# Moving the gate weights, the slot numbers and the first expert's conversions in an attention + mixture-of-experts + cosine-MLP kernel

## The chip, the cores and the metric

The kernel runs on one core of a Trainium2 chip. The metric is the device time of that core in microseconds (us); lower is better. The core's engines each run their own instruction stream in order: PE (matmuls; PEld is its weight load), DVE, ACT and POOL (elementwise work), and SP, which here only issues DMA loads and stores.

## The reference

Three stages follow each other: attention with queries averaged in pairs, a mixture of eight experts of which each token takes two, and a two-layer network with `h * cos(h)` between its layers. Shapes: 2 batches, 8 heads, 1152 keys, 576 pooled queries, head size 64; so 1152 tokens of 512 values.

```python
q_pool = q.reshape(B, H, S // 2, 2, D).mean(axis=3)
scores = scale * q_pool @ k.transpose(0, 1, 3, 2)
attn = softmax(scores)                       # over 1152 keys
x = (attn @ v).transpose(0, 2, 1, 3).reshape(1152, 512)

noisy = x @ w_gate + np.log1p(np.exp(x @ w_noise)) * noise   # 8 experts
top2 = the two largest of noisy; top2_w = softmax of the two
for e in range(8):                           # tokens that chose e
    out[mask] += top2_w * (np.maximum(x[mask] @ w1[e], 0) @ w2[e])

h = out @ w_in                               # 512 -> 2048
return (h * np.cos(h)) @ w_out               # 2048 -> 512
```

## The kernel before

Every product is done in split precision: a value is written as a high part, rounded to the type that PE multiplies fast, and a low part, the rest. `x_hi` or `conv` writes the high part (on ACT), the line after it the low part (mostly on DVE), and PE runs two or three products in place of one. The order of all work is written out by hand; each engine does its instructions in the order in which the program lists them.

**Attention.** 72 tiles of 128 queries (4 head pairs `hp`, 2 heads `hl`, 9 tiles) run in a loop over `n`. Iteration n emits the scores of tile n + 1 (`s_mm`, L302; maximum on DVE, L312; exponential on ACT, L321), the transposes of tile n (L336) and up to nine matmuls of earlier tiles with V (L374). A transposed tile goes to `eh` and `el` in three parts: two by ACT (L349) and DVE (L353), the third by `t_pool`: ACT copies it to `rw` (L357, two buffers), POOL makes `eh` (L359) and `el` (L360) of it. PE reads these a tile or two later. V is split on POOL too (`split_v`, L117 and L118), from `vn`, which SP loads (L111). What the next head pair needs is spread over the loop by `plan()`, which lists for each n the functions that run first in that iteration: `q_split` on POOL (L145, L147), `q_asm` (L154), `l_asm` (L162), `q_bd` (L170) and `k_asm` (L247), all loads from SP. The tile in the middle of a head (two batches) needs `kb` and `qd`; a head pair begins at n0 = 18 hp.

`load_gate` (L73, L79) runs once, at the end of the prologue: eight POOL instructions put identity blocks into `GW`, and eight loads on SP put the gate's and the noise's weights beside them, 8 columns each, by which `x_group` (L675) multiplies each finished head pair. The last prologue loads stand before it on SP, the loop's first load of `vn` behind it.

**Routing.** After the last tiles `route` runs in two halves, tokens tiles 0 to 3 (`ra`) and 4 to 8 (`rb`). It is a generator; `pump` advances it by a number of steps between other work. Its steps: log-probabilities on ACT and DVE (L467 to L476), the two largest (L479, L482), their one-hot codes `OH` (L484), 128 times the expert (`E128`, L486), the mask `MK` (L488), a matmul that counts earlier tokens of each expert (L496), `KEY` (L498), per token tile a comparison `PM` of the slot numbers with the token's slot in expert 0 (L502), and last the six instructions that work out every token's slot row (L505 to L514). PE then gathers expert 0's tokens with `hot` (L940): eight matmuls of each token tile's high and low parts with its `PM`. PE runs `hot(0, 3)` and `hot(1, 3)` of the first half, then the second half's counting matmul, then the rest.

**Experts.** Step s = 8 e + f handles an eighth of expert e: `h_mm` (twelve matmuls, L1102; ACT makes `hh`, L1113, DVE `hl`, L1114), and `yt_mm` for the step before (twelve matmuls, L1134). Weights come in units: even units 8 e + 2 i hold w1 for two steps, odd ones w2. SP loads a unit into one of three `raw` buffers (`raw_load`, L615 and L619), ACT writes its high part and DVE its low part (`conv`, L625 and L626), and only then is the raw buffer free for the unit three further on. `advance_c(c)` in step s converts up to unit c - 1 and loads up to three more; units 0 to 2 are converted on POOL during attention. The list in the loop gives c for steps 0 to 6, later it is s + 6 (s + 7 at the end). `slot_hots`, `slot_lo` (18 comparisons of DVE, L1064) and `slot_ids` (18 small matmuls, L1071, and six DVE instructions) make the table of which token stands in which slot; from it `x_load` (POOL, L1086) gathers an expert's tokens into three `xr` buffers, and `x_tr` (L1094) transposes them and splits them into `xe`. `yt_evac` copies a finished expert from PSUM (L1143 on ACT, L1145 on DVE), `yt_out` transposes it back (L1151). The last stage's weights come as 64-bit numbers: `dec_load` (L1173, L1175, 1 MB), decoding on DVE (L1182 to L1188) and a store by POOL (L1189), spread over the steps by `DECS`.

## Time and profile before

| | us |
|---|---|
| median of 3 runs | 753.76 (753.61 to 755.12) |
| the profiled execution | 753.42 |
| its span, first to last instruction | 751.8 |
| PE busy in the span | 730.8 |
| DVE busy | 561.8 |
| ACT busy | 519.9 |
| POOL busy | 295.2 |

The page gives the busy time of each engine. A busy PE is not a PE at its peak: its matmuls overlap and their ends are modelled. What is lost on PE shows in two ways, as idle time before an instruction with the name of what ended it, and as a longer distance between the starts of two matmuls than their kind needs. Attention takes about the first 275 us, routing the time to 297, the experts the time to about 545, the last network the rest.

### The profile page before, as it was taken

What the parts mean: (1) busy time and instruction counts of PE and PEld (TensorE: products, weight loads), DVE (VectorE), ACT (ScalarE), POOL (GpSimd) and SP (SyncE); (2) the same over time, 40 slices, a digit from 0 to 9 for tenths busy, and PEclk for the clock granted to TensorE, in tenths of its full rate; (3) what the DMA queues carried; (4) which work ended last, traced back from release to release, by engine and by line L of the source; (5) the groups of instructions that cost most, each with busy time, mean ns of one, the idle gap of its engine ahead of it and who ended that gap; (6) DMA issues with size and microseconds to landing.
All of it is one profiled execution on the core that took longest, in us unless ns stands there. A gap on an engine that the chain in (4) does not pass through costs nothing.

```text
span 751.8 us, 13714 instructions
## 1 busy us (share of the span) xinstructions
PE 730.8 (97%) x4803; PEld 676.7 (90%) x4803; DVE 561.8 (75%) x1176; ACT 519.9 (69%) x1193; POOL 295.2 (39%) x331
## 2 busy tenths in 40 slices
PE   7999999999999998999999999999999999999997
PEld 4789999999999998999999999999888999888885
DVE  5877878877888988868898887776667686656562
ACT  5988789879978963458776675766587675455443
POOL 5978767877877971122010220202177110000000
PEclk9999999999999999999999999999999999999999
DMA  9748667594745510778999999987464100010001
GB/s 219 167 108 214 150 150 164 122 250 98 179 109 171 176 43 19 256 234 287 377 321 348 351 334 325 316 276 236 144 180 137 57 28 1 1 43 0 2 0 60
DMA packets 75329, 125.02 MB, mean 166 GB/s; under 512 B 11950, under 2 KB 42030, under 8 KB 75254
## 3 DMA queue, kind: packets, MB, share of 16 engines
q1 hardware_dynamic: 68678, 101.92, 46.7%
q0 software_dynamic: 5568, 19.14, 7.6%
q10 hardware_dynamic: 1008, 3.02, 1.6%
q8 instruction: 40, 0.66, 0.4%
q14 instruction: 35, 0.29, 0.1%
HBM read 82.15 MB, written 20.33 MB: 136 GB/s over the span
## 4 chain that ended last, share of the span: by engine, by line
PE 77%; DMA 7%; DVE 6%; ACT 4%; POOL 2%; issue 2%; SPq 1%; ACTq 0%; DVEq 0%; POOLq 0%
PE h L1102 17%; PE acc L1102 13%; PE acc L1134 11%; PE s L302 10%; PE pa L374 8%; PE pt L336 8%; PE t L1102 6%; DMA raw<-w_d 2%; DMA qd<-ql 2%; DMA kb<-sh 1%; PE t L1094 1%; PE t L1151 1%; ACT u L625 1%; DMA xr<-x_d,NL 1%; PE pt L675 1%
## 5 line engine op out<-in xcount | busy, mean ns | idle before, releaser
L321 ACT ACTIVATE p<-s,nm 128x384 f32<-128x384 f32 x216 | 126.1, 593 | 0.9 <-DVE nm L314 0.5
L312 DVE TENSOR_REDUCE nm<-s 128x1 f32<-128x384 f32 x216 | 108.4, 550 | 22.9 <-PE s L302 22.3
L1102 PE MATMUL h<-xe,u 128*128 128x320 f32 (+5 forms) x768 | 120.4, 306 | 0.0
L1102 PEld LDWEIGHTS h<-xe,u 128*128 128x128 f32 x768 | 109.8, 189 | 0.5
L626 DVE TENSOR_TENSOR u<-raw,u 128x1024 fp32r<-128x1024 f32 x66 | 81.2, 1233 | 33.5 <-ACT u L625 33.3
L336 PE MATMUL pt<-ident,p 128*128 128x128 f32 x645 | 93.6, 273 | 0.5 <-ACT st L179 0.3
L302 PE MATMUL s<-kt,q 128*128 128x384 f32 x240 | 84.9, 370 | 2.6 <-DVE kt L193 1.3
L374 PE MATMUL pa<-eh,v 128*128 128x320 f32 (+1 forms) x279 | 86.6, 325 | 0.4 <-POOL eh L359 0.4
L625 ACT ACTIVATE u<-raw 128x1024 fp32r<-128x1024 f32 x73 | 77.1, 1058 | 11.3 <-DMA raw<-w_d 5.9
L349 ACT ACTIVATE eh<-pt 128x384 fp32r<-128x384 f32 x144 | 63.0, 492 | 31.1 <-PE pt L336 29.3
L374 PE MATMUL pa<-el,v 128*128 128x320 f32 (+1 forms) x279 | 82.4, 309 | 0.6 <-POOL el L360 0.6
L336 PEld LDWEIGHTS pt<-ident,p 128*128 128x128 f32 x645 | 77.7, 140 | 3.9 <-ACT st L179 0.6
L353 DVE TENSOR_TENSOR el<-pt,eh 128x384 fp32r<-128x384 f32 x144 | 73.1, 549 | 4.4 <-ACT eh L349 2.6
L360 POOL TENSOR_TENSOR el<-rw,eh 128x384 fp32r<-128x384 f32 x71 | 71.6, 1009 | 5.9
L1134 PE MATMUL acc<-hh,u 128*128 128x320 f32 (+5 forms) x448 | 71.8, 303 | 0.0
L1102 PE MATMUL acc<-u,gh 128*128 128x512 f32 x216 | 67.1, 392 | 0.3 <-ACT gh L1470 0.3
L1189 POOL DMA_DIRECT2D w_d<-dw x16 | 9.0, 563 | 148.0 <-DVE dw L1188 148.0
L302 PE MATMUL s<-kt,l 128*128 128x384 f32 x198 | 66.8, 340 | 0.0
L1134 PEld LDWEIGHTS acc<-hh,u 128*128 128x128 f32 x448 | 64.8, 188 | 0.0
L302 PEld LDWEIGHTS s<-kt,q 128*128 128x128 f32 x240 | 44.6, 190 | 11.2 <-ACT p L321 7.6
L374 PEld LDWEIGHTS pa<-el,v 128*128 128x128 f32 x279 | 52.9, 190 | 1.1 <-POOL el L360 1.1
L374 PEld LDWEIGHTS pa<-eh,v 128*128 128x128 f32 x279 | 52.9, 190 | 0.6 <-POOL eh L359 0.6
(285 smaller groups left out, 1599.3 us busy)
## 6 DMA issues: line engine op xcount, KB each, us to landing
raw<-in_moe_w_dram SPq DMA_DIRECT2D x64, 512.0 KB, 5.5
raw<-in_moe_w_in_dram SPq DMA_DIRECT2D x16, 512.0 KB, 7.8
raw<-in_moe_w_out_dram SPq DMA_DIRECT2D x16, 512.0 KB, 7.0
w_d<-dw POOLq DMA_DIRECT2D x16, 512.0 KB, 5.3
raw<-w_d SPq DMA_DIRECT2D x13, 512.0 KB, 3.7
vn<-in_v_dram SPq DMA_DIRECT2D x16, 288.0 KB, 4.9
q<-sh SPq DMA_DIRECT2D x14, 304.0 KB, 3.7
l<-ql SPq DMA_DIRECT2D x14, 304.0 KB, 4.3
```

The source lines that it names most:

```text
L302: nc.tensor.matmul(o, l, r, start=(m == 0), stop=(m == len(mm) - 1))
L312: nc.vector.tensor_reduce(NM[n][:, i:i + 1], SB[n][i][:, 0:384], axis=AX.X, op=OP.max, negate=True)
L321: nc.scalar.activation(P[n][i], SB[n][i][:, 0:384], AF.Exp, bias=NM[n][:, 3:4], accum_out=SUMS[:, t, 2 * hp + hl, i:i + 1])
L336: nc.tensor.transpose(p[:, c], P[n][j][:, c], ident)
L349: nc.scalar.activation(t_dst(n, j)[0], t_src(n, j), AF.Copy)
L353: nc.vector.tensor_tensor(el, t_src(n, j), ef, op=OP.subtract)
L360: nc.gpsimd.tensor_tensor(el, rw, ef, op=OP.subtract)
L374: nc.tensor.matmul(st["p"][:, 0:w], V2[hp, hl, b][:, VC[c] if hp + b else c, :], (EH, EL)[s][:, c, EB[g]:EB[g] + w], start=(c == 0 and s = ...
L625: nc.scalar.activation(b[:, 0], r, AF.Copy)
L626: st_w["lo"].tensor_tensor(b[:, 1], r, b.bitcast(F32)[:, 0], op=OP.subtract)
L1102: nc.tensor.matmul(o, l, r, start=first and i == 0, stop=last and i == len(seq) - 1)
L1134: nc.tensor.matmul(ACC[e, d][:, 0:CAPS[e]], w[:, i, 128 * d:128 * d + 128], r[:, 0:CAPS[e]], start=f == 0 and r is hh and i == 0, stop=f = ...
```

## The change

- `load_gate` leaves the end of the prologue and becomes the last event of iteration 8 in `plan()`, behind `q_split(1)`.
- `l_asm(hp, 1)` and `q_bd(hp, 1)` run in iteration n0 + 1 and no more in n0, so behind `k_asm(hp, 1)`.
- In `route` the product `E128` and the slot rows leave; a new function `slot_rows` does them once for all nine token tiles, right before `slot_hots`. For it ACT copies the counts from PSUM into `LG`, whose first eight columns are free by then. The `PM` comparisons of token tiles 1 to 3 move from DVE to POOL.
- `slot_lo` runs in steps 1 to 3 with three token tiles each; it ran in steps 0 to 3 with 3, 3, 2 and 1.
- `slot_ids` and `x_load(1)` run in step 4 ahead of the conversions and no more at its end.
- The conversions of steps 0 to 4 are one a step (units 3 to 7), two each in steps 5 and 6; they were 2, 0, 2, 1, 1, 1 and 2.
- The last product of expert 0, `yt_mm(0, 7)`, runs between the second and third transposes of expert 1 and no more ahead of them.
- `yt_evac(1)` is done by ACT alone.
- The second `dec_load` moves from step 3 to step 6.
- From expert 1 on `x_load(e + 2)` runs at f = 6, right after the transposes that free its buffers, and no more at the end of f = 7.

```diff
@@
                                 I8[:, ts, 0:2, None].to_broadcast([128, nt, 2, 8]), op=OP.is_equal)
-        nc.vector.tensor_scalar(E128[:, ts], I8[:, ts, 0:2], 128.0, None, op0=OP.mult)
         yield
@@
         nc.vector.scalar_tensor_tensor(KEY[:, ts], MK[:, ts, 0], -4096.0, pp[:, :, 0], op0=OP.mult, op1=OP.add)
+        nc.scalar.activation(LG[:, ts, 0:8], pp, AF.Copy)
         yield
@@
             PM[t] = xs.tile([128, CAP], F32R, name="pm", bufs=9)
-            nc.vector.tensor_scalar(PM[t], IOTAC, KEY[:, t:t + 1], None, op0=OP.is_equal)
+            eng = nc.gpsimd if 0 < t < 4 else nc.vector
+            eng.tensor_scalar(PM[t], IOTAC, KEY[:, t:t + 1], None, op0=OP.is_equal)
             yield
+
+    def slot_rows():
+        nt, ts = NT, slice(0, NT)
+        nc.vector.tensor_scalar(E128, I8[:, :, 0:2], 128.0, None, op0=OP.mult)
         tmp = OHP[:, ts]
-        nc.vector.tensor_tensor(tmp, OH[:, ts], pp[:, :, None, :].to_broadcast([128, nt, 2, 8]), op=OP.mult)
+        nc.vector.tensor_tensor(tmp, OH, LG[:, :, None, 0:8].to_broadcast([128, nt, 2, 8]), op=OP.mult)
         pj, pi = PJ[:, ts], PI[:, ts]
         nc.vector.tensor_reduce(pj, tmp, axis=AX.X, op=OP.add)
-        yield
         nc.vector.tensor_copy(pi, pj)
         nc.vector.scalar_tensor_tensor(pj, pj, 8.0, E128[:, ts], op0=OP.mult, op1=OP.add)
-        yield
         nc.vector.tensor_scalar(pi, pi, 127, None, op0=OP.bitwise_and)
-        yield
-        nc.vector.scalar_tensor_tensor(ROW[:, ts], pi, -7.0, pj, op0=OP.mult, op1=OP.add)
-        yield
+        nc.vector.scalar_tensor_tensor(ROW, pi, -7.0, pj, op0=OP.mult, op1=OP.add)
 
@@
                 at(m + 9 + d, q_asm, hp, 1, False)
-                at(n0, l_asm, hp, 1)
-                at(n0, q_bd, hp, 1)
                 for j in range(3):
@@
                 at(m + 18, k_asm, hp, 1)
+                at(n0 + 1, l_asm, hp, 1)
+                at(n0 + 1, q_bd, hp, 1)
+        at(8, load_gate)
         return ev
@@
     q_bd(0, 1)
-    load_gate()
 
@@
     def slot_lo(i):
-        for t in range((0, 3, 6, 8)[i], (3, 6, 8, 9)[i]):
+        for t in range(3 * i, 3 * i + 3):
             for j in range(2):
@@
             o = ACC.pop((e, d))[:, 0:n]
-            if d % 2 == 0:
+            if d % 2 == 0 or e == 1:
                 nc.scalar.activation(t[:, d, 0:n], o, AF.Copy)
@@
     CD = 5
-    DL = (1, 3)
+    DL = (1, 6)
     DECS = {}
@@
         DECS.setdefault(DL[i], []).append(lambda i=i: dec_load(i))
+    slot_rows()
     slot_hots()
@@
                 x_tr(e + 1, f - 3)
+                if f == 6 and e + 2 < E_N:
+                    x_load(e + 2)
             elif not e and f == 7:
-                yt_mm(0, 7)
                 for kd in range(4):
+                    if kd == 2:
+                        yt_mm(0, 7)
                     x_tr(1, kd)
@@
                 yt_evac(0)
+            if s == 4:
+                slot_ids()
+                x_load(1)
             if s < NCONV - 1:
-                advance_c((5, 5, 7, 8, 9, 10, 12)[s] if s < 7 else s + LA + (s > 58))
+                advance_c((4, 5, 6, 7, 8, 10, 12)[s] if s < 7 else s + LA + (s > 58))
             for c in DECS.get(s, []):
@@
             if not last:
-                if s < 4:
-                    slot_lo(s)
-                if (e, f) == (0, 4):
-                    slot_ids()
-                    x_load(1)
-                elif e and f == 7 and e + 2 < E_N:
-                    x_load(e + 2)
+                if 0 < s < 4:
+                    slot_lo(s - 1)
     for st in range(2):
```

## Rows read from the trace of the kernel before

**Rows 1.** Busy us of each engine in 38 windows of 20 us: their sum.
```profile
sum 760.00, PE 730.75 PEld 676.73 DVE 561.80 ACT 519.92 POOL 295.16; mean PE 19.23 PEld 17.81 DVE 14.78 ACT 13.68 POOL 7.77
```

**Rows 2.** PE's waits, by line and releaser: us in total, times, longest.
```profile
PE s L496 <- DVE MK L488: 1.0, 1, 1.0
...
PE pt L940 <- DVE pm L502: 0.8, 1, 0.8
PE acc L1134 <- DVE hl L1114: 0.7, 1, 0.7
PE s L302 <- DMA kb<-sh: 0.7, 2, 0.5
PE t L1094 <- DVE xe L989: 0.7, 1, 0.7
PE pa L374 <- POOL el L360: 0.6, 2, 0.3
PE t L1151 <- DVE yt L1145: 0.5, 1, 0.5
...
PE pa L374 <- POOL eh L359: 0.4, 1, 0.4
...
PE t L1094 <- DMA xr<-x_d,NL: 0.3, 1, 0.3
```

**Rows 3.** Timeline of PE, routing: start, us, instruction, count, idle before and releaser.
```profile
290.47 0.31 PE L940 MATMUL pa<-pm,xsh 128*128 128x320 f32 x1
290.62 0.31 PE L940 MATMUL pa<-pm,xsl 128*128 128x320 f32 x1
291.69 0.38 PE L940 MATMUL pt<-pm,xsh 128*128 128x320 f32 x1 [0.76 <-DVE pm L502]
```

**Rows 4.** Timeline of POOL, 24 to 56 us.
```profile
24.29 2.35 POOL L73 TENSOR_SCALAR GW<-ident 64x64 f32<-64x64 f32 x8
...
44.95 0.67 POOL L117 TENSOR_SCALAR v<-vn 128x576 fp32r<-128x576 f32 x1 [3.75 <-DMA vn<-in_v_dram]
...
54.91 1.01 POOL L360 TENSOR_TENSOR el<-rw,eh 128x384 fp32r<-128x384 f32 x1
```

**Rows 5.** ACT's waits between 24 and 58 us, by line and releaser.
```profile
ACT rw L357 <- POOL el L360: 1.6, 3, 0.7
```

**Rows 6.** Timeline of SP's issues, 35 to 53 us.
```profile
35.76 0.68 SPq L79 DMA_DIRECT2D GW<-in_moe_w_gate_dram  x1
...
41.16 0.55 SPq L111 DMA_DIRECT2D vn<-in_v_dram  x1
...
51.48 1.15 SPq L154 DMA_DIRECT2D q<-sh  x2
```

**Rows 7.** Timeline of SP's issues, start of the second head pair.
```profile
84.92 2.61 SPq L170 DMA_DIRECT2D qd<-ql  x2
```

**Rows 8.** Timeline of DVE in the routing.
```profile
282.55 0.39 DVE L502 TENSOR_SCALAR pm<-IOTAC,KEY 128x320 fp32r<-128x320 f32 x1 [0.39 <-DVE KEY L498]
...
289.29 0.21 DVE L505 TENSOR_TENSOR OHP<-OH,s 128x64 f32<-128x64 bf16 x1
```

**Rows 9.** Timeline of DVE and of POOL, step 0.
```profile
300.22 3.08 DVE L626 TENSOR_TENSOR u<-raw,u 128x1024 fp32r<-128x1024 f32 x2 [0.46 <-ACT u L625]
...
300.46 1.75 POOL L1058 TENSOR_TENSOR xr<-xr,M 128x432 bf16<-128x432 bf16 x1
```

**Rows 10.** The page's part 5: the group of low parts, count, busy us, mean ns.
```profile
L626 DVE TENSOR_TENSOR u<-raw,u 128x1024 fp32r<-128x1024 f32 x66 | 81.2, 1233 | 33.5 <-ACT u L625 33.3
```

**Rows 11.** Timeline of ACT and of PE, end of expert 0.
```profile
322.21 1.06 ACT L625 ACTIVATE u<-raw 128x1024 fp32r<-128x1024 f32 x1 [0.93 <-DMA raw<-in_moe_w_dram]
...
326.09 0.75 PE L1134 MATMUL acc<-hl,u 128*128 128x320 f32 x4
```

**Rows 12.** Loads of raw, issue to landing: 296 to 330 us, then to 525.
```profile
DMA to landing us min/median/max: 4.3/5.1/6.5
...
DMA to landing us min/median/max: 3.4/6.4/10.6
```

## The prediction

> **What bounds the kernel now.** I read each engine's busy time first: PE is busy 730.75 us of the span's 751.8, 97% [rows 1], and the chain that ended last runs mostly through PE, so the end moves only where PE stands still or is held back. Next came the list of PE's waits by line. Nine of its lines, 11 waits and 5.7 us in all, name a releaser that this change touches [rows 2]. The figure understates the loss, because a matmul's end is modelled: in the routing stretch the matmuls follow each other every 0.15 us, and then one start comes 1.07 us after the one before it (290.62 to 291.69). That is 0.92 us lost where the row shows 0.76 [rows 3]. I add this 0.16 us to each wait. The nine lines are then worth 5.7 + 11 x 0.16 = 7.5 us, which is about the most that the change can bring. Then I went to the timelines of POOL, SP, DVE and ACT around each wait, to see what was late and what will be late next.
>
> **Gate weights.** Three effects. (a) The eight builds of GW leave POOL at 24.29, where they take 2.35 us [rows 4]. Near there ACT waits three times, 1.6 us in all, for POOL to free `rw` [rows 5]. PE shows no wait for POOL there, only small ones for ACT, so this is worth between 0 and 1.2 us; I take 0.4, as ACT's wait reaches PE only in part. (b) The eight gate loads leave SP, where they run from 35.76 until the load of `vn` is issued at 41.16: 5.4 us [rows 6]. That load is what POOL waits 3.75 us for at 44.95 [rows 4]; its issue moves to about 35.8, it lands 3.8 us later at 39.6, and POOL, free at 41.20 now and 2.35 us sooner then, starts the split some 5.3 us earlier. The wait for `eh` (0.4) and one of two for `el` (0.3) follow this idle time [rows 2] and go: 0.7 + 2 x 0.16 = 1.0 us. (c) At step 8 the same builds and loads come back. On SP they are issued while it would wait until 51.48 for POOL's split of q [rows 6], so 5.4 us of issuing are covered; without that cover they would push all later loads back by 5.4 us. On POOL they stand between the q split and step 8's `el` (now 54.91 to 55.92, the second `el` wait) [rows 4]. POOL arrives up to 5.3 us earlier and loses 2.35 there, so this `el` is ready up to 3.0 us earlier while PE asks for it 1.0 us earlier. The wait (0.3 + 0.16) mostly goes; I take 0.3. Sum of (b) and (c): 1.3 us, from 0.3 (POOL still late) to 1.5.
>
> **l2 and qd one step later.** At the start of a head pair SP issues the two `qd` loads first, 2.61 us at 84.92 [rows 7], and then the loads of `kt` and `kb`. PE waits twice for `kb`, 0.7 us in all, 0.5 at most [rows 2]. Moving four loads behind brings `kb` forward by more than 2.61 us, five times the longest wait. What was moved is first used nine steps later. 0.7 + 2 x 0.16 = 1.0 us, from 0.4 to 1.2.
>
> **Routing.** On DVE three compares go to POOL, each of the kind at 282.55, 0.39 us, and the E128 product leaves the chain: 1.1 to 1.3 us less ahead of MK, for which PE waits 1.0 + 0.16 [rows 2, 8]. ACT's Ln, also needed, is done a little before that, so I leave 0.3 us of wait. The six slot instructions from 289.29 on, of 0.2 us each, 1.2 us, no longer stand ahead of tile 5's low part and compare [rows 8]; PE's wait for that compare, 0.8 + 0.16, goes entirely. Total 1.0 + 0.16 - 0.3 + 0.96 = 1.8, and 0.1 for E128 in the first half: 1.9 us. The added Copy on ACT falls where ACT has nothing to do. The compares on POOL have no row of before. Bounds for one: 0.3 us (a 64-wide build takes 2.35 / 8 [rows 4]) and 1.3 us (the slowest per element of POOL's rows here, 1.75 us for 432 [rows 9], times 320). The first compare, kept on DVE, ends at 282.94; PE spends 8 x 0.15 = 1.2 us per token tile, so it wants POOL's third at 286.5. Three at 1.3 us from 282.55 end at 286.45: hidden at either end; I take 1.0, nearer to the row of 432, whose width is nearer and which reads a second operand too. A second price: two low parts took 3.08 us on DVE while POOL ran a two-input operation from 300.46, against 1.23 us for one alone, so 0.6 us was lost to it [rows 9, 10]. The same may befall NL's products beside the compares: range of this part 1.0 to 2.3.
>
> On that row the Trainium skill (SBUF — State Buffer, Who interferes with whom) says that a DVE instruction with two SBUF inputs and a GpSimd instruction that reads SBUF exclude each other: whichever comes second stands until the first is done. The 3.08 us agree with it. By this rule NL's products could stand for one compare, 1.0 us as taken, and the time would be 748.0; by the clock of the rows POOL is done before them, and it stays at 747.0.
>
> **First expert.** The wait for `hl`, 0.7 + 0.16, comes from DVE doing two low parts in a row ahead of it (3.08 us [rows 9]) and then the first six table compares. With one conversion a step and no compares in step 0 it is early. But the slot instructions (six of 0.2 us [rows 8] and the E128 product, over 9 tiles at once: an estimated 1.5 us) and POOL's table operations now stand nearer to it: I take 0.7, from 0 to 0.9. Moving the last product of expert 0 between the transposes covers the wait for `xe`, 0.7 + 0.16. Against it: unit 8's conversion slips from step 4 to step 5, 24 matmuls at 0.15 or 3.5 us, and with it the raw buffer of unit 11, so that load is issued 3.5 us later against PE. ACT already waits 0.93 us for it before its conversion at 322.21, which ends at 323.27; the low part (1.23 [rows 10]) and `hl` (about 0.5) then end at 325.0, and PE needs this `hl` at 326.09 [rows 11]. Slack is 1.1 plus the 0.65 us by which the product moves back. This load landed after 6.4 us, where the raw loads of the first expert take 5.1 in the median and 6.5 at most [rows 12]; with the second double-precision load (1 MB) out of its way I expect the median: 3.5 - 1.3 - 1.75 = 0.45, say 0.5 us of new wait. Net 0.35 us, from -0.6 (landing unchanged, 6.4) to 0.85.
>
> **Later experts.** Evacuation of expert 1 on ACT alone removes the wait for `yt`, 0.5 + 0.16; ACT gets two more copies and DVE loses two: 0.6 (0.3 to 0.65). Gathers one step earlier remove the wait for `xr`, 0.3 + 0.16: 0.45 (0 to 0.5) [rows 2]; POOL waits for the transposes instead, and only a store of decoded weights is queued behind it.
>
> **Sum.** 0.4 + 1.3 + 1.0 + 1.9 + 0.7 + 0.35 + 0.6 + 0.45 = 6.7 us. The profiled execution took 753.4 us (span 751.8), which becomes 746.7; the runs' median is 0.3 above it, so **747.0**. All parts at their best make 9.1 us (744.7), all at their worst 1.4 us (752.4).
>
> **Rivals.** *Late load in the first expert.* If unit 11's load takes what the slowest raw load of the whole stage took, 10.6 us [rows 12], against the 5.1 assumed, its conversion, `hh` and `hl` move 5.5 us: 752.5; at 8 us it is 749.9. For it: more loads lie close together in steps 4 to 6. Against it: the gather of tokens is issued earlier, and no raw load of this stretch took over 6.5. Taken as 749.9 to 752.5.
>
> *The gate loads wait for POOL's builds.* They would then start only after POOL has done the q split, so after 51.48 [rows 6], and the builds, and whatever SP issues next comes 5.4 us or more later. How much of that reaches PE, no row tells: 0 to 5.4, I take half, 749.7. Against it: the eight loads now follow each other evenly, 5.4 us for eight, with no wait for POOL shown on SP.
>
> *Slower: the compares on POOL are far dearer than any of its rows.* Place: PE's matmuls of token tile 1 to 3 at 284 to 286.5. With p us for each, PE stands 3p - 4.0 us; the 1.9 us of the routing part are lost and its other waits (2.1) hide in this one. From 747.0: time = 747.0 + 1.9 - 2.1 + 3p - 4.0 = 742.8 + 3p. It is slower than before from p = 3.7, and by more than 0.2% from 4.2; at 5 us it makes 757.8. Rows bound p by 1.3. The Trainium skill (GPSIMD Engine Reference, 3.1 Elementwise — side-by-side cycle accounting) prices a data-dependent branch at about 12 cycles an element. If the compare were one, 320 elements at the page's 1.2 GHz would be an estimated 3.2 us and the time 752.4; no run here shows such an operation.
>
> **How the numbers follow.** Forecast as summed 0.78; late load 0.11; gate loads waiting 0.05; dear compares 0.06, half of it beyond 4.2 us, half somewhat below that and so within 0.2% of before. The range leaves out the dear compares, the upper half of the late loads and the very best sum: 744.3 to 750.4. A measurement of this kernel tells about 0.2% (1.5 us) from no change, so faster needs less than 752.25: the forecast, most of the late loads and the waiting gate loads, 0.93; same 0.04; slower 0.03.
>
> **What the new profile should show.** POOL without its 3.75 us idle before the first v split, PE without waits for `eh` near 47 and for `kb`; the wait for MK at most 0.3 us and none for the compare of tile 5; POOL's three compares at 0.3 to 1.3 us each; no wait for `hl` of step 1, `yt` of expert 1 and `xr` of expert 4. ACT should wait 1 to 2 us before the conversions of units 10 and 11. The prediction is wrong if PE waits over 1 us for `hh` or `hl` at the end of expert 0, or if a new wait for POOL follows step 8.

## The result and the profile after

| | before | after |
|---|---|---|
| median, us | 753.95 (753.5 to 755.12) | 747.41 (746.83 to 748.7) |
| the profiled execution | 753.42 | 746.88 |
| its span | 751.8 | 745.3 |

The ratio of the medians' runs is 0.9909 (95% interval 0.9896 to 0.9922). The forecast was 747.0, within 744.3 to 750.4.

The busy time of the engines in the changed kernel, over its whole span (compare [rows 1]; 11 windows, so only the sums compare), and below it those of PE's waits that name a line of the change (compare [rows 2]):

```profile
sum 746.00, PE 727.94 PEld 676.68 DVE 559.50 ACT 520.24 POOL 302.53; mean PE 66.18 PEld 61.52 DVE 50.86 ACT 47.29 POOL 27.50
```

```profile
PE t L1095 <- DMA xr<-x_d,NL: 1.3, 1, 1.3
...
PE pa L374 <- POOL el L360: 0.4, 1, 0.4
```

The nine lines of [rows 2] were worth 5.7 us. One is left whole, the `el` behind step 8, and one that was 0.3 us at expert 4 is now 1.3 us at another place: the transposes of expert 1. (Lines of code from about 490 on stand one or two further down in the changed kernel: L1094 is L1095 there, L1114 is L1115, L626 is L627.)

Where the time went can be read exactly. Both traces hold the same 4803 matmuls in the same order, except around the first transposes, so each matmul of one can be set against the same matmul of the other: its start before less its start after is the lead that PE has won by then. The first 31 us hold nothing of the change but scatter from one execution to the next (last section), so the lead is counted from the matmul that starts at 31.64 us before and at 31.47 after.

| matmul that starts, before, at | after | lead, us | won since | by |
|---|---|---|---|---|
| 31.64 | 31.47 | 0 | | (0.17 of scatter left out) |
| 40.66 | 40.38 | 0.11 | 0.11 | builds off POOL at 24 |
| 49.46 | 47.90 | 1.40 | 1.29 | V split early: waits for `eh`, `el` |
| 56.44 | 55.22 | 1.05 | -0.35 | `el` of step 8 |
| 96.75 | 94.74 | 1.84 | 0.79 | `kb`, second pair |
| 162.88 | 160.35 | 2.36 | 0.52 | `kb`, third pair |
| 281.65 | 279.09 | 2.39 | 0.03 | |
| 288.49 | 284.85 | 3.46 | 1.07 | MK |
| 294.71 | 289.81 | 4.74 | 1.28 | compare of tile 5 |
| 306.77 | 300.86 | 5.74 | 1.00 | `hl` of step 1 |
| 319.34 | 313.45 | 5.72 | -0.02 | |
| 333.73 | 328.35 | 5.22 | -0.50 | end of expert 0 |
| 360.76 | 354.44 | 6.16 | 0.94 | `yt` of expert 1 |
| 373.07 | 367.29 | 5.61 | -0.55 | `hh` and `hl` behind it |
| 428.55 | 422.20 | 6.18 | 0.57 | `xr` of expert 4 |
| 510.83 | 504.46 | 6.21 | 0.03 | |
| 578.45 | 571.74 | 6.54 | 0.33 | network, not touched |
| 745.79 | 739.08 | 6.53 | 0 | |

**Gate weights.** POOL in the changed kernel (start, us, instruction, idle before; compare [rows 4]):

```profile
39.31 0.67 POOL L117 TENSOR_SCALAR v<-vn 128x576 fp32r<-128x576 f32 x1
...
45.03 0.51 POOL L359 TENSOR_SCALAR eh<-rw 128x384 fp32r<-128x384 f32 x1 [1.97 <-PE s L302]
...
46.60 1.22 POOL L145 TENSOR_SCALAR sh<-st 128x1216 fp32r<-128x1216 f32 x1
...
50.66 2.35 POOL L73 TENSOR_SCALAR GW<-ident 64x64 f32<-64x64 f32 x8
53.09 0.51 POOL L359 TENSOR_SCALAR eh<-rw 128x384 fp32r<-128x384 f32 x1
53.69 1.00 POOL L360 TENSOR_TENSOR el<-rw,eh 128x384 fp32r<-128x384 f32 x1
```

The split of V starts at 39.31 without idle time; it was 44.95 behind 3.75 us of it. POOL then stands 1.97 us before 45.03, although the row names PE: the `rw` that this `eh` reads is copied by ACT just before (ACT, same kernel).

```profile
44.45 0.50 ACT L357 ACTIVATE rw<-pt 128x384 f32<-128x384 f32 x1
```

The eight builds, 2.35 us, now stand right ahead of `eh` and `el` of step 8, and PE waits for that `el` (PE, same kernel):

```profile
53.89 0.49 PE L336 MATMUL pt<-ident,p 128*128 128x128 f32 x3
54.75 0.39 PE L374 MATMUL pa<-el,v 128*128 128x256 f32 x1 [0.37 <-POOL el L360]
```

**Routing.** POOL's three compares, then PE at the counting matmul and at tile 5's compare (compare [rows 3]):

```profile
279.70 3.42 POOL L503 TENSOR_SCALAR pm<-IOTAC,KEY 128x320 fp32r<-128x320 f32 x3 [1.06 <-DVE KEY L497]
```

```profile
284.32 0.31 PE L941 MATMUL pt<-pm,xsl 128*128 128x320 f32 x1
284.75 0.18 PE L495 MATMUL s<-MK,LT 128*128 128x40 bf16 x1
...
286.99 0.31 PE L941 MATMUL pa<-pm,xsl 128*128 128x320 f32 x1
287.13 0.31 PE L941 MATMUL pt<-pm,xsh 128*128 128x320 f32 x1
```

A compare takes 1.15 us on POOL. The counting matmul follows 0.43 us behind the one before it, 0.28 more than the 0.15 of its neighbours; that distance was 1.32 before. The matmul of tile 5 that had come 1.07 us late comes after 0.14.

**End of expert 0.** PE, and ACT in the same stretch:

```profile
319.03 0.38 PE L1095 MATMUL t<-ident,xr 128*128 128x128 f32 x2
320.69 0.66 PE L1095 MATMUL t<-ident,xr 128*128 128x128 f32 x4 [1.29 <-DMA xr<-x_d,NL]
321.11 1.42 PE L1135 MATMUL acc<-hh,u 128*128 128x320 f32 x8
```

```profile
314.68 1.06 ACT L626 ACTIVATE u<-raw 128x1024 fp32r<-128x1024 f32 x1 [0.24 <-DMA raw<-in_moe_w_dram]
318.05 1.06 ACT L626 ACTIVATE u<-raw 128x1024 fp32r<-128x1024 f32 x1 [2.32 <-DMA raw<-in_moe_w_dram]
319.02 0.42 ACT L1114 ACTIVATE hh<-h 128x320 fp32r<-128x320 f32 x1
```

Two transposes run, then PE stands 1.29 us (1.53 between starts) until the third gather of tokens has landed, at 320.65. The next product, eight matmuls on `hh` and four on `hl`, finds both ready. ACT waits 0.24 us for unit 10's load and 2.32 us for unit 11's.

### The profile page after: what moved, and what is told of

Same layout as the page of the kernel before. It is cut to its first block, busy times and chain, and to the rows that moved or that the text cites. A ratio compares the mean times of both kernels' runs of the same rounds, so it can differ in the third digit from the quotient of the medians.

```text
span 745.3 us, 13708 instructions
## 1 busy us (share of the span) xinstructions
PE 727.9 (98%) x4803; PEld 676.7 (91%) x4803; DVE 559.5 (75%) x1164; ACT 520.2 (70%) x1197; POOL 302.5 (41%) x334
## 4 chain that ended last, share of the span: by engine, by line
PE 77%; DVE 5%; ACT 4%; DMA 4%; issue 3%; POOL 3%; SPq 3%; ACTq 0%; POOLq 0%; DVEq 0%
PE h L1103 17%; PE acc L1103 14%; PE acc L1135 9%; PE s L302 9%; PE pa L374 8%; PE pt L336 7%; PE t L1103 6%; PE pt L676 2%; DMA raw<-in_moe_w_dram 1%; PE t L1095 1%; PE t L1152 1%; ACT p L321 1%; DMA xr<-x_d,NL 1%; ACT u L626 1%; DVE nm L312 1%
## 5 line engine op out<-in xcount | busy, mean ns | idle before, releaser
L627 DVE TENSOR_TENSOR u<-raw,u 128x1024 fp32r<-128x1024 f32 x66 | 80.9, 1227 | 33.4 <-ACT u L626 33.3
L626 ACT ACTIVATE u<-raw 128x1024 fp32r<-128x1024 f32 x73 | 77.0, 1056 | 12.7 <-DMA raw<-in_moe_w_dram 7.0
L359 POOL TENSOR_SCALAR eh<-rw 128x384 fp32r<-128x384 f32 x71 | 36.4, 513 | 43.9 <-ACT rw L357 41.9
```

Of the source, the lines that this page charges most:

```text
L626: nc.scalar.activation(b[:, 0], r, AF.Copy)
L627: st_w["lo"].tensor_tensor(b[:, 1], r, b.bitcast(F32)[:, 0], op=OP.subtract)
```

## The experiments

Leads are counted as above, from the matmul that starts at 31.64 us in the kernel before; "ahead of the changed kernel" is the difference of two such leads. How sharp that is depends on the place. From 281.65 to 294.71 the nine kernels with the changed kernel's routing win 2.33 to 2.35 us each. In attention the kernels with the changed kernel's order agree within 0.05 us at 49.46 and within 0.33 at 281.65. Those that keep the old order there do not: with nothing changed in attention, the kernel with the routing edits alone leads the kernel before by 0.36 us at 49.46 and by 0.71 at 281.65, and the one with the later `l2` and `qd` has lost 0.96 at 49.46, ahead of its edit. The attention figures, taken against the one profile of the kernel before, are therefore good to some tenths of a microsecond and that of the V split to about one. No run has the edit of `yt`, the gathers from expert 1 on, the conversions of the first steps or the later table alone; what is said of these is read from the leads.

### The gate weights alone

```diff
-    load_gate()            # end of the prologue
+        at(8, load_gate)   # plan()
```

> The kernel before with one edit: the gate weights' builds and loads move from the prologue to step 8. My theory (terms a to c of the prediction): POOL's 3.75 us of idle time before the split of v at 44.95 goes, and PE's waits for eh near 47 and el near 48.5 with it; the matmuls that start at 89.82 us in the kernel before should start 1.2 to 1.3 us earlier, as they do in the changed kernel (1.26), and that lead should still be there at the end: about 752.5 us against 753.95. The two waits for kb (0.5 and 0.2 us) stay. Rival 1, the loads wait for POOL's builds and push SP's later loads back: a lead under 0.6 us at 89.82, and a wait of PE for a load of v or k after step 8. Rival 2, the lead is given back at a later wait: 1.2 us at 89.82 and less than 0.4 at 281.

Measured: 752.59 us, ratio 0.9974 (0.9955 to 0.9992). The lead is 1.39 us at 49.46 and 1.06 at 56.44, the changed kernel's within 0.01; 1.03 at 89.82 (1.2 to 1.3 were expected); 1.40 at 281.65, as the two waits for `kb` shrink (0.4 us left of 0.7; they were expected to stay, and in the kernel with the routing alone, whose SP order is the old one, 0.3 is left, so this is within their scatter). It stays 1.40 until 419, and then 0.68 is lost in one place (PE):

```profile
426.23 0.38 PE L1094 MATMUL t<-ident,xr 128*128 128x128 f32 x2
427.60 0.33 PE L1094 MATMUL t<-ident,xr 128*128 128x128 f32 x1 [1.00 <-DMA xr<-x_d,NL]
```

The theory holds for terms (a) and (b). Term (c) does not: 0.33 us is lost at step 8 as in the changed kernel, which is why the lead at 89.82 falls short. Rival 1 is out. Rival 2 has a point of its own, if later than it said: half of the lead goes where the gather for expert 4 is late, so that 0.63 of 1.40 is left at the end. That wait was 0.3 us before [rows 2]; the third gather is issued 1.3 us earlier here (418.79 against 420.07) and PE gets it only 0.5 us earlier. In the changed kernel, where these gathers start one step sooner, nothing is lost there. The kernel with the routing alone loses 0.46 us there too. So that edit is worth more than the wait that it removes: it lets the other leads through.

### l2 and qd alone

```diff
-                at(n0, l_asm, hp, 1)
-                at(n0, q_bd, hp, 1)
+                at(n0 + 1, l_asm, hp, 1)   # behind k_asm(hp, 1)
+                at(n0 + 1, q_bd, hp, 1)
```

> The kernel before with one edit: the assembly of l2 and qd of the second half pair is one step later (18 hp + 1). My theory: the two qd loads were 2.6 us of issuing ahead of kt and kb; without them both waits of PE for kb go, and the second pair's matmuls start 0.7 to 0.8 us earlier after 95 us, 1.2 to 1.3 us after 162 us, nothing else changes: about 752.7 us. Rival: the waits for kb went in the changed kernel because POOL and SP were earlier after the move of the gate weights; then both waits stay here, and the lead at 281 us is under 0.3 us.

Measured: 753.55 us, ratio 0.9985 (0.9965 to 1.0005). Both waits for `kb` are gone; the lead grows by 0.74 us at 96.75 and by 0.54 at 162.88, 1.28 together, as the changed kernel's does (1.27 from 89.82 on). The theory holds and the rival falls, although the size is not as sharp: in the same stretch the kernel with the routing alone, which has no such edit, wins 0.33 us. The interval of the ratio takes in 1, so the runs' times alone show no gain. The profiled run shows less than the edit gives because it lost 0.96 us earlier, where it does not differ from the kernel before in a single instruction:

```profile
PE pa L374 <- POOL eh L359: 1.3, 1, 1.3
```

The load of `vn`, issued at 41.76, kept POOL idle for 4.71 us instead of 3.75 [rows 4]. What the old order costs there is thus not 1.3 us but a figure that moves by a microsecond from one execution to the next: set against this profile the new order wins 2.2 us between 40.66 and 49.46, against that of the routing alone 1.0.

### The routing alone

The edits of `route`, `slot_rows` and the call of it, and nothing of the first expert's schedule.

> The kernel before with the routing edits alone: compares of tiles 1 to 3 on POOL, the slot numbers computed at once after the routing, E128 with them. My theory: the wait for MK falls from 1.17 us between starts to about 0.3, the wait for tile 5's compare (0.92) goes, so the first product of expert 0 starts 1.9 to 2.4 us earlier; POOL's compares take 1.1 to 1.2 us each. What stands behind them moves against step 1: the table of step 0 is still there, so the wait for hl of step 1 (0.91) stays or grows to at most 1.5. The lead at the slot table's matmuls (313.9 in the kernel before) is 1.6 to 2.4 us, about 752.0 us in all. Rival A: the slot numbers, now between routing and the first expert, cost there what they gave: lead under 1.2 us. Rival B: the wait for hl goes here too, so the routing edits and not the conversions removed it: lead above 2.8 us.

Measured: 752.41 us, ratio 0.9968 (0.9954 to 0.9981). From 281.65 to 294.71 the lead grows by 2.22 us (changed kernel: 2.35). Then 0.63 is lost again (PE):

```profile
301.81 1.34 PE L1135 MATMUL acc<-hh,u 128*128 128x320 f32 x8
304.53 0.85 PE L1135 MATMUL acc<-hl,u 128*128 128x320 f32 x4 [1.38 <-DVE hl L1115]
```

The wait for `hl` of step 1, 0.7 us before [rows 2], is 1.38. The slot numbers are not free: they push 0.63 us into the first expert, and only in the changed kernel, with the new conversion list and the later table, are that and the old wait gone, 1.63 us in all by this kernel's measure; which of the two does it no run separates. Rival B is out, and A too: of the lead of 2.30 at the slot table 0.71 was there before the routing, so the edits keep 1.6. The theory's "stays or grows to at most 1.5" is what happened.

### The compares back on DVE

```diff
-            eng = nc.gpsimd if 0 < t < 4 else nc.vector
-            eng.tensor_scalar(PM[t], IOTAC, KEY[:, t:t + 1], None, op0=OP.is_equal)
+            nc.vector.tensor_scalar(PM[t], IOTAC, KEY[:, t:t + 1], None, op0=OP.is_equal)
```

> The changed kernel with the compares of tiles 1 to 3 back on DVE. My theory: three compares of 0.39 us, which overlap a little, stand ahead of MK again, so the wait for MK grows from 0.29 to between 0.9 and 1.3 us between starts, and tile 5's compare is not waited for, since the slot numbers are still behind: PE is 0.6 to 1.0 us behind the changed kernel from there on, about 748.2 us. Rival A: ACT's Ln, not DVE, sets MK: less than 0.2 us lost. Rival B: it was the compares, and not the slot numbers, that held tile 5: a wait of 0.5 us or more for pm of tile 5 comes back as well, 1.5 us or more lost.

Measured: 749.4 us, ratio 0.9915 (0.9885 to 0.9945). It falls 0.82 us behind the changed kernel between 281.65 and 288.49, at one matmul, and under 0.1 more up to 353 us:

```profile
285.53 0.31 PE L940 MATMUL pt<-pm,xsl 128*128 128x320 f32 x1
286.78 0.18 PE L495 MATMUL s<-MK,LT 128*128 128x40 bf16 x1 [0.94 <-DVE MK L487]
```

So DVE sets MK and the three compares are worth 0.82 us there. Tile 5's wait stays away here too, so the move of the slot numbers is enough to remove it.

### Gate weights at step 7

```diff
-        at(8, load_gate)
+        at(7, load_gate)
```

> The changed kernel with the gate weights at step 7 instead of 8. The prediction held that POOL's eight builds (2.35 us with their gaps) cost nothing at step 8; in the changed kernel they stand from 50.66 to 53.0 right ahead of eh and el of 53.1 to 54.7, and PE waits 0.54 us for this el. My theory: at step 7 they fall in POOL's 1.97 us of idle time before 45.03, so the wait for el goes or falls under 0.2, at the price of up to 0.4 us for eh at 45; POOL's split of q still starts after ACT's st at 46.6. The lead at 56 us over the changed kernel: 0.3 to 0.6 us. Rival: the wait of 0.54 does not come from the builds but from the split of q (2.8 us) ahead of them, as in the kernel before (0.44 there): then it stays, and the lead is under 0.15 us or negative.

Measured: 748.15 us in one execution, whose first 31 us took 1.0 us longer than the changed kernel's. From there it is 0.87 us ahead at 56.44 (0.3 to 0.6 were expected) and 0.4 to 0.5 from 89.82 on to 320. POOL, and PE at the `el` of step 8:

```profile
44.07 2.36 POOL L73 TENSOR_SCALAR GW<-ident 64x64 f32<-64x64 f32 x8
46.52 0.52 POOL L359 TENSOR_SCALAR eh<-rw 128x384 fp32r<-128x384 f32 x1
...
52.76 1.01 POOL L360 TENSOR_TENSOR el<-rw,eh 128x384 fp32r<-128x384 f32 x1
```

```profile
54.66 0.49 PE L336 MATMUL pt<-ident,p 128*128 128x128 f32 x3
54.91 0.36 PE L374 MATMUL pa<-el,v 128*128 128x256 f32 x1
```

PE goes from one line to the other without a wait. It was the builds, not the split of q, that held this `el`; in POOL's idle time before 45.03 they cost PE nothing.

### The product ahead of the transposes

```diff
+                yt_mm(0, 7)
                 for kd in range(4):
-                    if kd == 2:
-                        yt_mm(0, 7)
                     x_tr(1, kd)
```

> The changed kernel with the last product of expert 0 ahead of all transposes again, as before. There PE loses 1.66 us at the first transposes (319.14), where the prediction had none. Theory G, the gathers: the third gather of tokens for expert 1 lands at 320.65, and the transposes now come 1.8 us earlier than behind the product. Then this kernel's transposes start at about 321 and wait for no gather; instead PE waits 0.4 to 0.5 us for hh of step 7 (ACT stands for the raw load of unit 11 until 318.05) and 0.8 to 0.9 for xe, as in the kernel before: 0.2 to 0.5 us gained on the changed kernel behind the transposes. Rival L, the prediction's own late load: PE is held because unit 11's conversion, and with it hh and hl, is late; then the product waits over 1 us here, and nothing is gained or more is lost.

Measured: 747.84 us in one execution. PE:

```profile
319.70 1.44 PE L1135 MATMUL acc<-hh,u 128*128 128x320 f32 x8 [0.17 <-ACT hh L1114]
...
321.74 0.81 PE L1095 MATMUL t<-ident,xr 128*128 128x128 f32 x6
323.20 0.90 PE L1095 MATMUL t<-ident,xr 128*128 128x128 f32 x6 [0.65 <-DVE xe L990]
```

No wait for a gather is left, as theory G says: the transposes simply came before their tokens. In its place stand, between starts, 0.34 us for `hh`, 0.85 for `xe` and some tenths in small steps. From 319 us to behind the transposes the kernel loses 0.1 us on the changed one; 0.2 to 0.5 of gain were expected. Rival L is half right: with the gathers' wait gone, `hh` behind unit 11 is next in line, if only by 0.34.

### Unit 11 one step later, and the product cut

```diff
-                advance_c((4, 5, 6, 7, 8, 10, 12)[s] if s < 7 else s + LA + (s > 58))
+                advance_c((4, 5, 6, 7, 8, 10, 11)[s] if s < 7 else s + LA + (s > 58))
```

> The changed kernel with unit 11's conversion one step later (behind hh of step 7 on ACT instead of ahead of it). Theory G, the gathers: PE's wait of 1.3 us for xr at the first transposes stays, within 0.3 us, and the time of the whole is that of the changed kernel within 0.4 us. Rival L, the late load of unit 11: the loss of 1.66 us behind 319 falls to under 0.6, and the whole gains about 1 us. Either way ACT's wait of 2.3 us for that load no longer stands ahead of hh of step 7.

The second kernel has this edit too, and cuts the product:

```diff
                 for kd in range(4):
+                    if kd == 0:
+                        yt_mm(0, 7, (0, 1))   # the eight matmuls on hh
                     if kd == 2:
-                        yt_mm(0, 7)
+                        yt_mm(0, 7, (2,))     # the four on hl
                     x_tr(1, kd)
```

> The changed kernel with unit 11's conversion one step later, and the last product of expert 0 cut in two: its eight matmuls on hh (1.2 us) ahead of the transposes, its four on hl between the second and the third group of transposes. Theory G, the gathers: 1.2 of the 1.66 us are covered, so PE waits 0.2 to 0.5 us for xr, none or up to 0.3 for xe, and what follows starts 1.0 to 1.2 us earlier than in the changed kernel: about 745.8 us, if nothing later gives it back (the stretch from 332 to 450, where DMA is busy 0.97 of the time, may do so). Rival L, the late load: as without the cut, PE gains about 1 us from the later conversion, and the wait for xr goes whether the product is cut or not.

Measured: 751.1 and 750.92 us, one execution each. Both miss what was expected of waits and time; only that `hh` of step 7 no longer stands behind unit 11 came true (at 317.88 in the first, without a wait for a load). They fall 3.9 and 2.1 us behind the changed kernel between 319 and 353 us. PE's waits in the first (us in total, times, longest):

```profile
PE t L1095 <- DMA xr<-x_d,NL: 1.9, 1, 1.9
```

In the second nothing is lost at the transposes (0.9 us for `xr`, 0.1 us ahead by 329), and all of it at 336 and 338, where PE waits for `hh` and `hl` and 2.1 us go by the leads. The edit moved more than it named. A conversion frees a raw buffer, so SP's list of loads moved with it: the load of unit 14 left step 6, the 1 MB double-precision load behind it came some 3 us earlier (317.71 in the first, changed kernel 320.82), among the gathers and the load of unit 11, and unit 11 itself was converted only at 327.35, behind the evacuations of `xe`. The two kernels say nothing on G against L, but they show what one step of a load can cost here: 2 to 4 us, of which about 1.6 in the first are the clock, as told below (from 321.73 on sixteen matmuls that take 2.26 us in the changed kernel take 3.83).

### Unit 8 one step earlier; the 1 MB load earlier; all together

```diff
-                advance_c((4, 5, 6, 7, 8, 10, 12)[s] if s < 7 else s + LA + (s > 58))
+                advance_c((4, 5, 6, 7, 9, 10, 12)[s] if s < 7 else s + LA + (s > 58))
```

> The changed kernel with the conversion of unit 8 back in step 4 (two conversions there, one in step 5). The prediction priced its move to step 5 as 3.5 us later for the load of unit 11. Theory, both mechanisms real: the raw load of unit 11 is issued about 0.9 to 1.2 us earlier than in the changed kernel (DVE's and ACT's order and the landing of unit 8's own load allow no more), hh of step 7 comes at 318 instead of 319.0, ACT's wait of 2.3 us for that load falls to 1.3 or less; but PE still stands 1.2 to 1.6 us for the third gather at the first transposes, so the whole is within 0.4 us of the changed kernel from 24 us to 340 us. Rival: the gathers land late because they share DMA with these loads; then the wait for xr moves by over 0.5 us with the loads, up or down.

```diff
-    DL = (1, 6)
+    DL = (1, 3)
```

> The changed kernel with the second double-precision load (1 MB) back in step 3. The prediction let unit 11's load land in 5.1 us instead of 6.4 because this load is out of its way; in the changed kernel it took 4.9. Theory: with it in step 3 the gathers and the raw loads of units 10 to 12 land 1 to 2 us later, PE's wait for xr at the first transposes grows from 1.3 to between 2 and 3 us, the whole is 1 to 2 us slower. Rival: DMA has room there (0.77 to 0.90 busy), landings move under 0.5 us and the time is the same within 0.4 us.

The third kernel has the gate weights at step 7, the conversion list of the first diff and the cut product.

> The changed kernel with three edits: gate weights at step 7, unit 8's conversion in step 4, and the last product of expert 0 cut in two around the first transposes (eight matmuls on hh before them, four on hl in the middle). Theory: the first gives 0.5 us by 90 us as it did alone; the second keeps hh and hl of step 7 in time (318.7 and 319.9 on the changed kernel's clock), which they were not in the run with the late conversion of unit 11; the third covers 1.2 of 1.6 us of the wait for the gather. In all 1.0 to 1.5 us before the changed kernel from 24 us to 330 us, about 746 us. Rival: the low parts of units 7 and 8 in a row make DVE late for hl of step 5 or 6, as two in a row did for hl of step 1 in the kernel before; then a wait for hl of 0.5 us or more shows between 312 and 316, and the gain is under 0.5 us.

Measured: 748.39, 750.26 and 747.18 us, one execution each. The loads of the stretch, from the trace, in us on the changed kernel's clock (each kernel's times moved by its distance to the changed one at 313.45: -0.10, -0.98 and 0.56 us); unit 11's landing is the start of its conversion on ACT, which waits for it:

| kernel | third gather issued, landed | unit 11's load issued, landed | ahead of the changed kernel at 319, at 334 |
|---|---|---|---|
| changed | 314.26, 320.65 | 313.16, 318.05 | 0, 0 |
| unit 8 earlier | 313.64, 320.80 | 312.17, 318.68 | -0.07, -0.24 |
| 1 MB load in step 3 | 314.26, 320.83 | 313.16, 320.76 | -0.06, -2.71 |
| all together | 313.63, 321.04 | 312.19, 319.68 | 0.51, -0.44 |

Unit 11's load, issued 1.0 us earlier, lands 0.6 or 1.6 us later, and a gather issued 0.6 us earlier lands 0.15 or 0.4 later. So an earlier issue of unit 11 did not bring its `hh` earlier in either kernel, though the whole of the first stays within 0.4 us of the changed kernel as expected. Within such bounds the issue does not set the landing here; that what else is in flight does is argued, not shown, except for the 1 MB load. With all together the wait for the gather is gone and PE waits longer for `hh`, behind unit 11:

```profile
PE acc L1136 <- ACT hh L1114: 1.9, 1, 1.9
```

It loses the 0.51 us that the gate weights had brought and 0.44 more; its rival (a wait for `hl` between 312 and 316) is not what did it. With the 1 MB load back in step 3, unit 11's load is issued at the same moment and lands 2.7 us later, and PE loses 2.65 us (1 to 2 were expected):

```profile
320.01 0.27 PE L1095 MATMUL t<-ident,xr 128*128 128x128 f32 x1
321.28 0.33 PE L1095 MATMUL t<-ident,xr 128*128 128x128 f32 x1 [1.01 <-DMA xr<-x_d,NL]
321.86 0.66 PE L1095 MATMUL t<-ident,xr 128*128 128x128 f32 x4 [0.25 <-DMA xr<-x_d,NL]
323.18 2.17 PE L1135 MATMUL acc<-hh,u 128*128 128x320 f32 x8 [0.66 <-ACT hh L1114]
```

The waits in these lines cost about 1.1 us more than the changed kernel's. The rest, 1.6 us, is the clock. The eight matmuls on `hh` take 2.17 us, 1.42 in the changed kernel: from 323.58 to 326.21 PE starts ten matmuls in 2.63 us, where 0.147 each make 1.47, and four transposes behind them take 0.83 us instead of 0.43. In windows of 2 us (PE busy, its count, ..., granted clock, DMA share, GB/s):

```profile
321.00:323.00 2.00, 0.98 (x5) 0.56 (x5) 1.18 (x2) 1.26 (x2) 0.00 (x0) 1.00 0.43 140
323.00:325.00 2.00, 1.82 (x8) 1.82 (x9) 2.00 (x4) 0.71 (x3) 0.00 (x0) 0.65 0.72 253
325.00:327.00 2.00, 2.00 (x10) 1.96 (x9) 0.17 (x1) 0.00 (x0) 0.00 (x0) 0.50 0.89 256
```

After 321 to 323, in which PE was busy half the time, the granted clock fell from 1.00 to 0.50, the lower level of 1.2 GHz, until 327. The kernel with unit 11 one step later shows the same between 321.7 and 325.3 (granted 0.70 and 0.50 in the windows from 321 and 323); in the changed kernel PE is busy 0.71 of 2 us from 319 to 321 and the clock stays at 1.00. So the theory is right that the 1 MB load delays unit 11, and wrong on the way: the third gather lands 0.2 us later and the wait for it does not grow; the loss is `hh` behind unit 11, and the clock. Of the parts tried around the first expert the later 1 MB load is worth most, 2.65 us, and the prediction had it only as the reason for unit 11's shorter landing.

### ACT's order alone

```diff
             h_mm(e, f)
+            if s == 7:
+                advance_c(12)      # unit 11, behind hh of step 7
+                dec_load(1)        # from DL, so the order of loads stays
-    DL = (1, 6)                    # its second load
-                advance_c((4, 5, 6, 7, 8, 10, 12)[s] if s < 7 ...
+                advance_c((4, 5, 6, 7, 8, 10, 11)[s] if s < 7 ...
-        at(8, load_gate)
+        at(7, load_gate)
```

and the cut product.

> The changed kernel with gate weights at step 7, the last product of expert 0 cut in two around the first transposes as before, and ACT's order alone changed at step 7: hh of step 7 first, then unit 11's conversion, both ahead of the transposes, and the second double-precision load right behind it on SP, so that no load moves against the gathers. Theory: three things lay one on the other behind 319 us, the gathers (third landing near 320.6 however early they were issued, since DMA is full), ACT standing for unit 11's load in front of hh, and the evacuation of xe; hh is now ready at 318, so the eight matmuls on hh cover 1.2 of the 1.6 us of the wait for xr, and PE loses 0.4 to 0.7 us in all between 319 and the first product of expert 1, against 1.4 in the changed kernel. With 0.5 us from the gate weights the lead over the changed kernel from 24 us to 330 us is 1.2 to 1.6 us, the median about 746.1 us. Rival: DMA decides alone; then unit 11's load, conversion or hl comes later by what PE gains, a wait for hl or xr of about 1.3 us stays, and the lead is that of the gate weights, 0.5 us.

Measured: 746.14 us (745.56 to 747.7), ratio to the kernel before 0.989 (0.9865 to 0.9914). PE at the end of expert 0:

```profile
319.18 1.34 PE L1136 MATMUL acc<-hh,u 128*128 128x320 f32 x8
320.36 0.93 PE L1095 MATMUL t<-ident,xr 128*128 128x128 f32 x6
321.04 0.83 PE L1136 MATMUL acc<-hl,u 128*128 128x320 f32 x4
321.93 0.90 PE L1095 MATMUL t<-ident,xr 128*128 128x128 f32 x6
```

No wait is marked in these lines; at 328 us the kernel is 1.36 us ahead of the changed one, as the theory has it. Some ten microseconds later that is given back (ACT, then PE):

```profile
334.31 1.06 ACT L626 ACTIVATE u<-raw 128x1024 fp32r<-128x1024 f32 x1 [1.87 <-DMA raw<-in_moe_w_dram]
...
337.44 1.06 ACT L626 ACTIVATE u<-raw 128x1024 fp32r<-128x1024 f32 x1 [1.48 <-DMA raw<-in_moe_w_dram]
```

```profile
338.18 0.80 PE L1136 MATMUL acc<-hl,u 128*128 128x280 f32 x4 [0.40 <-DVE hl L1115]
...
341.31 0.91 PE L1136 MATMUL acc<-hh,u 128*128 128x280 f32 x5 [0.46 <-ACT hh L1114]
```

The load issued at 326.17 takes 8.1 us; the same one in the changed kernel, issued at 327.10, takes 6.6, and there ACT waits only 0.3 us in all between 330 and 343. At 347 us the lead is 0.04, and 0.1 from 367 on. The rival, that DMA decides alone, fits this better than the theory, though the wait appears 15 us later than it said and most of the gate weights' 0.5 us goes with it; one trace does not show that nothing else plays a part. By the medians this version is 1.3 us below the changed kernel, but the two ratios' intervals overlap almost wholly and the traces show a lead of 0.1 us at most past 347 us: it is not shown to be faster.

## Why the prediction was right

The sum was 6.7 us against the profiled execution; the last matmul comes 6.70 us earlier, the execution is 6.54 shorter. The total is closer than its terms, and that is luck: four terms fall short of the forecast by 1.9 us in all, five exceed it by 1.45, and 0.4 comes from places that the change does not touch.

| step of the prediction | forecast | measured |
|---|---|---|
| (a) builds off POOL at 24 | 0.4 | 0.2 |
| (b) V split early | 1.0 | 1.3 |
| (c) builds and loads at step 8 | 0.3 | -0.35 |
| `l2` and `qd` later | 1.0 | 1.3 |
| routing | 1.9 | 2.35 |
| `hl` of step 1 | 0.7 | 1.0 |
| product between the transposes, late load | 0.35 | -0.5 |
| `yt` of expert 1 on ACT | 0.6 | 0.4 |
| `xr` of expert 4 | 0.45 | 0.55 |

(For (a): 0.11 after 31.64, and 0.06 between there and 24 us, by the leads of the two matmuls. The rest of the 6.7 is 0.33 in the network, where other kernels with the same code lie up to 1.1 us behind the changed one, and 0.1 of scatter.)

**What held.** The method did: nine waits, each with the engine that is late before it. Seven of the nine lines go or become small; of the other two one wait stays and one comes new elsewhere. V's split starts 5.64 us earlier, forecast 5.3. The gate loads on SP follow each other at step 8 from 38.13 to 44.31, and SP then waits for the q split until 47.84: covered, as forecast, so the rival in which they wait for POOL did not happen. `kb`, MK, tile 5, `hl`, `yt` and `xr` of expert 4 went as named, MK to 0.28 (at most 0.3 was forecast). Unit 11's load is issued 3.25 us later against PE (3.5 forecast) and takes 4.9 us (5.1); with the 1 MB load back in step 3 it takes 7.6. ACT's wait of 2.32 us for it is a little over the 1 to 2 forecast.

**The compares.** 1.15 us each against 1.0 taken and bounds of 0.3 and 1.3; the dear compare (from 3.7 us on) did not happen. The Trainium skill (GPSIMD Engine Reference, 3.1 Elementwise — side-by-side cycle accounting), from whose price for a branch 3.2 us had been estimated, is not borne out for this operation by the 1.15 us. Of the lock between DVE and POOL that the Trainium skill states (SBUF — State Buffer, Who interferes with whom) the routing shows little, and the measurement decides: beside the third compare the product of L474 takes 0.42 us on DVE, 0.19 before, so 0.23 instead of the 1.0 that it could have cost, and the two products of L469 and L470 beside the second compare take 0.20 each, as before.

**Step (c) failed.** It let POOL come to step 8 up to 5.3 us earlier. POOL came to the builds at 50.66, and the split of q ahead of them started only 3.65 us earlier than before (46.60 against 50.25), because the `eh` and `el` ahead of it wait for ACT's `rw`: 1.97 us of POOL's gain stood as idle time before 45.03. After the builds `el` starts 1.22 us earlier (53.69 against 54.91), while PE is 1.56 us earlier by then. The wait that should "mostly go" grew from 0.44 to 0.54 us between starts, and 0.23 for the `eh` ahead of it came new. A new wait for POOL behind step 8 was one of the two things by which the prediction called itself wrong; for this step it is. With the builds at step 7 all of it is gone; 0.4 to 0.5 us of that stay.

**The end of expert 0 failed.** The step weighed the product's cover against the late load of unit 11 and forecast 0.35. It left out a third thing that the same edit does: the transposes come 1.8 us earlier against their gathers, the third of which lands after 6.4 us here. Before, it landed at 326.07, 0.6 us ahead of the first transposes at 326.68; that slack was not looked up. Nor is this gather issued earlier, as the prediction took it to be: 314.26 is 320.15 on the clock of the kernel before, where it was also 320.15. The first one is 1.2 us earlier, but the first two hold POOL for 1.89 and 1.58 us instead of 1.20 and 1.07 (last section). The lower end of the step, -0.6 for a landing of 6.4 us, does not follow from its own numbers either: 3.5 - 1.75 against 0.86 makes -0.9. In most kernels of the last sections the three waits at this place (gather, `hh` behind unit 11, `xe`) are alternatives: take one away and another is there, at once or, with ACT's order alone, 15 us later. That the loads set this sum is the reading that fits them; it is not isolated. An exact term was not to be had from the wait list.

**`yt`.** The wait went (0.9 us by the leads); then 0.26 was lost to `hh` at 358, which ACT, with two extra copies ahead of it, reaches later, and 0.34 to `hl` at 366.8, behind a load that took 9.4 us. The second did not recur in the kernels that keep this code (they regain 0.2 to 0.35 us on the changed kernel there), so 0.6 was a fair value for the edit.

## What to carry to other kernels

Set the same matmul of two traces against each other: the lead over time shows, edit by edit, what was won and what was given back, often at a tenth of a microsecond, where whole runs scatter by one. Check first how far two kernels with the same code at that place differ: here between 0.02 us in the routing and 1 us where V is loaded in the old order. Moving a conversion or a load also moves every load that waits for its buffer; write out the queue that results before you price the step. In a stretch where many loads are in flight (in the changed kernel a 512 KB load takes 3.4 us when issued at 306.23 and 6.6 at 314.29, beside the gathers) taking away one wait may bring up the next; what helped here was to move 1 MB behind the gathers.

## What was not expected of the hardware

**After some of PE's waits the lower clock is granted, after others not.** In two kernels PE's waits near 321 us were followed by some 4 us at 1.2 GHz, and that cost 1.6 us, more than the added waits themselves. It does not come with every wait: in the kernel with all three edits together PE stands longer at one place, 1.93 us, and the granted clock stays at 1.00:

```profile
319.00:321.00 2.00, 0.45 (x3) 0.45 (x4) 0.79 (x1) 1.38 (x2) 0.00 (x0) 1.00 0.75 271
321.00:323.00 2.00, 2.00 (x17) 1.96 (x15) 1.04 (x3) 0.65 (x2) 0.00 (x0) 1.00 0.29 46
```

What decides between the two is open. The start of the executions scatters too: the matmul that starts at 31.64 us before starts between 31.42 and 32.93 in the 14 profiles, though only POOL's builds at 24 us differ ahead of it, and that is as much as the larger terms of the sum. In the kernel with unit 11 later and the product cut, where it is last, the lower level was granted from 12 to 20 us:

```profile
12.00:16.00 4.00, 3.21 (x16) 2.20 (x15) 3.03 (x7) 1.51 (x8) 2.25 (x3) 0.50 1.06 334
```

In the changed kernel it was granted for a part (0.80 from 12 to 16, 0.78 from 16 to 20), and with all three edits together, where that matmul is first (31.42), not at all. But the kernel with the gate weights at step 7 alone shows 1.00 throughout these windows and is among the late ones (32.47), so the granted clock does not account for the whole scatter.

**A gather's issue gets longer by what DVE's low part has left.** The three gathers of expert 1 hold POOL for 1.89, 1.58 and 0.94 us in the changed kernel. The first two start while a low part runs on DVE, the third while `hl` is about to. POOL's second gather and DVE's low parts:

```profile
312.37 1.58 POOL L1087 DMA_INDIRECT xr<-x_d,NL  x1 [0.30 <-issue]
311.90 2.36 DVE L627 TENSOR_TENSOR u<-raw,u 128x1024 fp32r<-128x1024 f32 x2 [0.46 <-ACT u L626]
```

In the kernel with unit 8 earlier, the second gather meets no low part at its start and takes 0.96, and the third, which starts 0.62 us into the low part at 313.12, 1.43. The 546 gathers of the 14 profiles agree with this, but for one. DVE's 128x1024 instructions with two inputs (low parts and the decoding) take about 1.2 us; the 370 gathers that start while none of them runs take 0.94 to 1.20 us (median 0.95), whether one begins a little later or not. Of those that start inside one, the 26 with 0.2 to 0.4 us of it left take 1.2 in the median, the 40 with 0.6 to 0.8 left 1.57, the 37 with more than 1.0 left 1.96: what is left of it and then about 0.9. This is read from the traces; no kernel took the low parts away. It matters for the change: with `x_load(1)` ahead of the conversions the first gather is issued 1.2 us earlier, but the low parts then hold the first two, and the third is no earlier than before.
